# Taps to 128 partitions, a band in 128x32 tiles, first weights as fp32: the start of a convolution and gated feed-forward kernel

## The chip, the cores and the metric

The kernel runs on one core of a Trainium2 chip. The metric is the device time of one execution in microseconds. Before the change it is 761.82 us, the median of three runs (761.52 to 762.06). Beside the times there is a profile of one execution, taken by the hardware profiler.

## The reference

Two stages follow each other. The first is a causal convolution of seven taps over time, with one set of taps for each of 8 heads of 24 channels, the taps made to sum to one by a softmax. The second is a feed-forward block with a ReLU gate:

```python
w = weight - np.max(weight, axis=-1, keepdims=True)      # weight: 8 x 7
w = np.exp(w)
w = w / (np.sum(w, axis=-1, keepdims=True) + 1e-09)
x_pad = zeros of 6 steps ahead of x                       # x: 8 x 4096 x 192, fp32
out = np.einsum('hk,bskhg->bshg', w, x_unf)               # x_unf: 7 shifted views of x_pad
x = out.reshape(32768, 192)
gate = np.maximum(x @ w_gate, 0.0)                        # w_gate, w_val: 192 x 1536
val = x @ w_val
result = (gate * val @ w_out)                             # w_out: 1536 x 192
```

All inputs and the result are fp32.

## The kernel before, in words

**Tiling.** The batch is cut into two streams of four sequences, which lie in partitions 0 to 63 and 64 to 127; the 192 channels are three chunks of 64. A unit `u` is 1024 steps of both streams, two windows of 512 (`WIN`). There are 16 units. For each, `gate_val` (L601) runs over 12 blocks `f` of 128 columns of the gate and value weights: TensorE multiplies (L621), ScalarE takes the ReLU of the gate from PSUM (L632), VectorE multiplies by the value product (L633). Then `project_turn` (L636) multiplies by `w_out`, VectorE transposes out of PSUM (L661), and SyncE stores. The convolution of later units is done beside it by ScalarE, VectorE and GpSimd as seven scaled additions (`lane_first`, `lane_rest`, `product`, `add`).

**The first unit.** Its convolution can't wait for that lane, so TensorE does it, as a product of x with a band matrix: `band(h)` is 118 rows by 112 columns and holds the taps of head `h` along its diagonals. Window 0 is cut into five steps of 106 columns (`STEP`; the last has 88), each read from its own rows of x. `load_raw` (L106) requests the five loads of x for both streams as fp32, four by SyncE in the order 1, 0, 3, 4 and number 2 by ScalarE; `cast` (L118) turns them to fp16 on ScalarE in the order `STEPS0 = [1, 0, 2, 3, 4]`. `conv_steps` (L377) multiplies one step for one chunk of channels: eight small products in 128x32 tiles of the TensorE array. Chunk `c` needs heads up to 2, 5 and 7. The results are evicted from PSUM by `evict` (L401) into `dense[0]`, which the gate products of `f = 0` then read, chunk by chunk.

**The band.** The 8x7 taps are loaded into `w8` (L129). A product with `rows8` (L203), a 0/1 matrix made by GpSimd's `affine_select`, spreads each head's taps over 16 partitions into the PSUM tile `spread`. VectorE takes the maximum `mx` (L275), ScalarE the exponential `e` (L278) and the sum (L281), VectorE forms `prod`, `blk`, the reciprocal `sm` and three groups of `blocks` (L287 to L299), one group for heads 0 to 2, 3 to 5, and 6 to 7. TensorE raises each group to a band in PSUM, eight products of 128x128 a group (L335), each placed 16 steps further; zero products (L209) have cleared the banks. VectorE casts each band to fp16 (L343). GpSimd makes `wn`, the normalised taps (L308), for the lane's tap table, which SyncE then copies by small DMAs (L354).

**Idle products.** `hold` (L191) has TensorE multiply ones ahead of the first real work, in groups given by `WARM`: 13 times 128 columns before L203 and 9 times 128 after it.

**Weights.** Gate and value weights are cast to fp16 by GpSimd's DMAs (`load_w`, L221) in four groups of columns: 0 to 128, to 384, to 768, to 1536 (`CUTS`), gate and value alternating. They land in partitions 0 to 63; a copy to partitions 64 to 127 (`both_halves`, L229) is made by VectorE for the first two 128 columns, by GpSimd (`pool_halves`) for those to 1280, by SyncE's DMA for the rest. A one-element memset of `Wg` by VectorE (L178) stands ahead of GpSimd's first weight load, which writes over the same element and so waits for it.

**What sets the order.** Each engine runs its instructions in program order; the framework adds the semaphores. GpSimd's order is: small setup, weight groups 0 and 1, `wn`, weight groups 2 and 3, copies, the first stream of x for window 1 (`load_x(1, ...)`, L97), copies, the second stream, copies, and the loads of the lane. Window 1's convolution by TensorE comes after block `f = 9` of window 0 (`CONV1`). PSUM tiles named `ps` rotate through four buffers of two banks.

## Time and profile before

| | |
|---|---|
| median of 3 runs | 761.82 us |
| span of the profiled execution, first to last instruction | 760.2 us |
| granted TensorE clock, mean | 1.000 |
| TensorE busy | 756.0 us, 99% |
| VectorE, ScalarE, GpSimd busy | 675.8, 610.1, 461.3 us |
| first gate product (L621) starts | 7.81 us |
| convolution of window 1 (L391) starts | 20.96 us |
| HBM read and written | 28.98 and 25.17 MB |

The profiled execution has no other time of its own than its span, which is 1.6 us less than the median; what lies ahead of the first instruction and behind the last is not in it. In the views, PE is TensorE, PEld its weight load, DVE is VectorE, ACT ScalarE, POOL GpSimd and SP SyncE; a `q` behind the name marks the issue of a DMA. L12 is line 12 of the kernel before. A row of the timeline has start, duration, engine, line, operation, output and input, and in brackets how long the engine was idle and what it waited for. The chain of waits is followed back from the last instruction, at each step to what let it start. Busy shares are averages; where nearly all of the span is one engine's work, what is left to look at are the microseconds in which that engine does something else.

### The profile page before, as it was taken

How to read it: one execution, taken by the hardware profiler on the slowest of the kernel's cores; microseconds unless marked ns; L12 is line 12 of the kernel's file. 1: busy time of each engine (PE TensorE's matmuls, PEld its weight loads, DVE VectorE, ACT ScalarE, POOL GpSimd, SP SyncE). 2: the span in 40 equal slices, each digit the busy share in tenths (PEclk: the TensorE clock that was granted, in tenths of full speed). 3: DMA queues.
4: the chain of work that ended last, by engine and by line, in shares of the span. 5: the costliest groups of instructions: out<-in, count | busy, mean ns of one | idle time of the engine just before them, and what ended most of it. 6: DMA issues, size and time to landing. Idle time of an engine off the chain costs nothing.

```text
span 760.2 us, 30531 instructions
## 1 busy us (share of the span) xinstructions
PE 756.0 (99%) x13724; PEld 454.8 (60%) x13724; DVE 675.8 (89%) x647; ACT 610.1 (80%) x680; POOL 461.3 (61%) x311
## 2 busy tenths in 40 slices
PE   9999999999999999999999999999999999999998
PEld 5555555565565666656666565666656556566658
DVE  7889989998998989989999899998999989897891
ACT  7897887878878788887877878788797887877671
POOL 8729649195591946829377392874919659193600
PEclk9999999999999999999999999999999999999999
DMA  8953532345324443333434324352243531240302
GB/s 142 137 69 92 79 85 46 43 96 75 85 44 52 97 66 85 55 61 83 60 85 71 66 67 55 85 85 69 56 49 93 77 86 44 23 100 9 85 2 85
DMA packets 153714, 54.07 MB, mean 71 GB/s; under 512 B 148912, under 2 KB 153584, under 8 KB 153584
## 3 DMA queue, kind: packets, MB, share of 16 engines
q1 hardware_dynamic: 117376, 37.78, 21.6%
q0 software_dynamic: 35808, 14.07, 16.4%
q8 instruction: 107, 1.75, 1.0%
q10 hardware_dynamic: 400, 0.27, 0.1%
q14 instruction: 23, 0.19, 0.1%
HBM read 28.98 MB, written 25.17 MB: 71 GB/s over the span
## 4 chain that ended last, share of the span: by engine, by line
PE 99%; DMA 0%; ACT 0%; issue 0%
PE ps L621 65%; PE ps L643 31%; PE ps L686 2%; PE ps L391 0%; DMA w<-in_weight_dram 0%; PE ps L193 0%; PE ps L335 0%; PE ps L414 0%; PE ps L209 0%; PE ps L203 0%; ACT out_s L697 0%; ACT L127 0%
## 5 line engine op out<-in xcount | busy, mean ns | idle before, releaser
L633 DVE TENSOR_TENSOR hT<-gr,ps 128x1024 f16<-128x1024 f16 (+1 forms) x385 | 469.1, 1219 | 35.5 <-ACT gr L632 8.7
L632 ACT ACTIVATE gr<-ps 128x1024 f16<-128x1024 f32 (+1 forms) x385 | 392.8, 1021 | 114.4 <-PE ps L621 114.4
L550 POOL TENSOR_TENSOR prod<-prod,prod 128x896 f32<-128x896 f32 x145 | 302.6, 2087 | 251.8 <-DVE prod L584 242.7
L621 PE MATMUL ps<-xc,Wg 64*64 64x512 f16 (+1 forms) x4464 | 318.4, 376 | 0.0
L621 PE MATMUL ps<-xc,Wv 64*64 64x512 f16 (+1 forms) x4464 | 318.3, 376 | 0.0
L643 PE MATMUL ps<-hT,Wo 64*64 64x512 f16 x4320 | 235.8, 376 | 0.0
L621 PEld LDWEIGHTS <-Wv 64*64 64x64 f16 (+1 forms) x4464 | 149.9, 106 | 98.5 <-DVE hT L633 0.3
L621 PEld LDWEIGHTS <-Wg 64*64 64x64 f16 (+1 forms) x4464 | 145.4, 107 | 103.4 <-issue 0.2
L643 PEld LDWEIGHTS <-Wo 64*64 64x64 f16 x4320 | 137.3, 107 | 95.7
L538 ACT ACTIVATE prod<-x_r,tap 128x1024 f32<-128x1024 f16 (+2 forms) x195 | 182.7, 1017 | 0.0
L574 DVE SCALAR_TENSOR_TENSOR acc<-x_r,tap,acc 128x1024 f32<-128x1024 f16 (+3 forms) x150 | 118.0, 854 | 0.0
L661 DVE STREAM_TRANSPOSE out_s<-ps 128x1024 f32<-128x1024 f32 x45 | 56.2, 1248 | 28.4 <-PE ps L643 24.4
L550 POOL TENSOR_TENSOR xc<-prod,prod 128x896 f16<-128x896 f32 x29 | 60.6, 2089 | 2.3
L479 POOL COPY x_p<-x_e 128x1536 f16<-128x1536 f16 (+1 forms) x32 | 42.2, 1351 | 0.0
L251 POOL DMA_DIRECT2D x_e<-in_x_dram x30 | 26.6, 890 | 0.0
L574 DVE SCALAR_TENSOR_TENSOR xc<-x_r,tap,acc 128x1024 f16<-128x1024 f16 (+3 forms) x30 | 25.2, 840 | 0.0
L563 ACT ACTIVATE acc<-x_r,tap 128x1024 f32<-128x1024 f16 (+3 forms) x30 | 22.5, 800 | 0.0
L656 ACT COPY turned_by<-ps 128x2 f32<-128x2 f32 x45 | 7.0, 155 | 16.8 <-PE ps L643 14.8
L686 PEld LDWEIGHTS <-hT 128*128 128x128 f16 x192 | 15.8, 98 | 0.4 <-issue 0.4
L686 PE MATMUL ps<-Wo,hT 128*128 128x192 f16 x192 | 16.0, 246 | 0.0
L697 ACT COPY out_s<-ps 128x768 f32<-128x768 f32 (+2 forms) x5 | 3.2, 638 | 12.7 <-PE ps L686 12.7
L697 DVE COPY out_s<-ps 128x192 f32<-128x192 f32 x1 | 0.4, 359 | 13.3 <-PE ps L686 13.3
(61 smaller groups left out, 74.4 us busy)
## 6 DMA issues: line engine op xcount, KB each, us to landing
out_dram<-out_s SPq DMA_DIRECT2D x125, 192.0 KB
x_e<-in_x_dram POOLq DMA_DIRECT2D x28, 384.0 KB, 6.3
x_r<-x_p SPq DMA_TRANSPOSE x116
prod<-in_moe_w_out_dram POOLq DMA_DIRECT2D x1, 576.0 KB, 8.7
prod<-in_x_dram SPq DMA_DIRECT2D x3, 168.0 KB
out_dram<-out_s SPq DMA_DIRECT2D x5, 96.0 KB
out_s<-in_x_dram POOLq DMA_DIRECT2D x2, 210.0 KB, 6.2
out_s<-in_x_dram POOLq DMA_DIRECT2D x2, 192.0 KB, 6.1
```

Source lines behind the costliest of these rows:

```text
L251: nc.gpsimd.dma_start(out=xe[:, 0:n, st, :, :].rearrange("p j c r -> p j (c r)"), in_=bass.AP(tensor=x.tensor, offset=x.offset + row * D, ...
L479: nc.gpsimd.tensor_copy(out=xp[:, js, :, st, :], in_=xe[:, js, st, :, :])
L538: nc.scalar.activation(out=both(prods[b, k], b, at, n), in_=shifted(b, c, k, t, n), func=ACTF.Copy, scale=tap[:, c, k : k + 1],)
L550: nc.gpsimd.tensor_tensor(out=acc if k < KW - 1 else xcs[b][:, w, :, :].rearrange("p c t -> p (c t)")[:, LDVE : NCH * WIN], in0=acc, in1=p ...
L563: nc.scalar.activation(out=both(accs[b], b, at, n), in_=shifted(b, c, 0, t, n), func=ACTF.Copy, scale=tap[:, c, 0:1],)
L574: nc.vector.scalar_tensor_tensor(out=result(b, at, n) if k == KW - 1 else both(acc, b, at, n), in0=shifted(b, c, k, t, n), scalar=tap[:, c ...
L621: nc.tensor.matmul(out=pss[i][q : q + M, st, :], lhsT=W[64 * st : 64 * st + 64, c, 128 * f + q : 128 * f + q + M], rhs=xcb[64 * st : 64 * ...
L632: nc.scalar.activation(out=gr[:, sts], in_=pss[0][:, sts], func=ACTF.Relu)
L633: nc.vector.tensor_tensor(out=h[:, f, sts], in0=gr[:, sts], in1=pss[1][:, sts], op=ALU.mult)
L643: nc.tensor.matmul(out=ps[64 * st : 64 * st + 64, b, :], lhsT=Wo[64 * r : 64 * r + 64, f, p, :], rhs=hs[b][64 * r : 64 * r + 64, f, st, :] ...
L661: nc.vector.transpose(out=o[:].rearrange("p t (b d) -> p b t d", b=2)[:, :, :, 32 * p : 32 * p + 32], in_=ps[:].rearrange("p b (t c) -> p ...
L686: nc.tensor.matmul(out=ps[:, i // 2, D * (i % 2) : D * (i % 2) + D], lhsT=h[:, f, st, 128 * q : 128 * (q + 1)], rhs=Wo[:, f, :, :].rearran ...
```

## The change: what it does

- The taps are requested by one DMA straight into 128 partitions, each head's row repeated 16 times. `rows8`, its select and the product into `spread` go; `mx` and `e` read the loaded tile. The two groups of idle products become one of 22 times 128 columns.
- The band products write 32 partitions each, in 128x32 tiles, in the order `PLACED`, two for each group of 32 partitions.
- In the convolution of window 0, step 4 of chunks 0 and 1 comes after the four other steps of both. The evictions of chunks 0 and 1 are split at column 318 (`early_cols`, `late_cols`) between VectorE and ScalarE.
- The first 128 columns of both weights come as fp32 by four DMAs into `sent`, all 128 partitions, the gate's by SyncE and the value's by ScalarE, behind the loads of x. VectorE casts them into `Wg` and `Wv`. GpSimd no longer loads group 0; the memset's element moves to column 128, the first of group 1.
- The first stream of x for window 1 is requested after GpSimd's copies up to column 768 instead of after those up to 384.

```diff
-    WARM = [(4, 4, 4, 1), (4, 4, 1)]
+    WARM = (4, 4, 4, 4, 4, 2)
     STEPS0 = [1, 0, 2, 3, 4]
+    PLACED = [0, 2, 4, 6, 1, 3, 5, 7]
...
-    w8 = const.tile([H, KW], FP)
-    nc.scalar.dma_start(out=w8[:], in_=weight)
+    w = const.tile([128, KW], FP)
+    nc.scalar.dma_start(
+        out=w[:],
+        in_=bass.AP(
+            tensor=weight.tensor, offset=weight.offset, ap=[[KW, H], [0, 128 // H], [1, KW]]
+        ),
+    )
     for jj in (1, 0, 3, 4):
         load_raw(nc.sync, jj)
     load_raw(nc.scalar, 2)
+    sent = apool.tile([128, 2 * LPOOL], FP, name="prod6")[:, 0 : 2 * NCH * 128].rearrange(
+        "p (i c f) -> p i c f", i=2, c=NCH
+    )
+    for i, (queue, src) in enumerate(((nc.sync, moe_w_gate), (nc.scalar, moe_w_val))):
+        for half in (slice(0, 64), slice(64, 128)):
+            queue.dma_start(
+                out=sent[half, i],
+                in_=src.rearrange("(c p) f -> p c f", p=64)[:, :, 0:128],
+            )
...
-    rows8 = const.tile([H, 128], FP)
-    select(rows8[:], H, [[-1, H], [0, HR]])
...
-    nc.vector.memset(Wg[0:1, 0, 0:1], 0.0)
+    nc.vector.memset(Wg[0:1, 0, 128:129], 0.0)
...
-    spread = psum.tile([128, 2, 512], FP, name="ps")
-    hold(*WARM[0])
-    nc.tensor.matmul(out=spread[:, 0, 0:KW], lhsT=rows8[:], rhs=w8[:], start=True, stop=True)
-    hold(*WARM[1])
+    hold(*WARM)
...
-    for s in range(2):
-        load_w(s)
+    load_w(1)
...
-        out=mx[:], in_=spread[:, 0, 0:KW], axis=mybir.AxisListType.X, op=ALU.max, negate=True
+        out=mx[:], in_=w[:], axis=mybir.AxisListType.X, op=ALU.max, negate=True
     )
-    nc.scalar.activation(out=e[:, 0:KW], in_=spread[:, 0, 0:KW], func=ACTF.Exp, bias=mx[:])
+    nc.scalar.activation(out=e[:, 0:KW], in_=w[:], func=ACTF.Exp, bias=mx[:])
...
     pool_halves(2)
-    xts[1] = load_x(1, range(1))
     for s in (3, 4, 5):
         pool_halves(s)
+    xts[1] = load_x(1, range(1))
     load_x(1, range(1, 2))
...
-        for j in range(128 // HR):
+        for j in PLACED:
+            q = HR * j // 32 * 32
...
-                lhsT=Z[:, 112 - HR * j : 240 - HR * j],
+                lhsT=Z[:, 112 - HR * j + q : 144 - HR * j + q],
...
-                stop=(j == 128 // HR - 1),
+                stop=(j % 2 == 1),
+                tile_position=(0, q),
...
-    def evict(copy, g, ps, c):
-        copy(out=dense[0][:, g, c, :], in_=ps[:, 0, :])
+    def evict(copy, g, ps, c, cols=slice(0, WIN)):
+        copy(out=dense[0][:, g, c, cols], in_=ps[:, 0, cols])
...
-    for c, steps in ((0, STEPS0[:3]), (1, STEPS0[:2]), (0, STEPS0[3:]), (1, STEPS0[2:]), (2, STEPS0)):
+    for c, steps in ((0, STEPS0[:4]), (1, STEPS0[:4]), (0, STEPS0[4:]), (1, STEPS0[4:]), (2, STEPS0)):
         conv_steps(0, first[c], c, steps)
-    both_halves(nc.vector.tensor_copy, 0, Wg)
-    both_halves(nc.vector.tensor_copy, 0, Wv)
-    for c, copy in enumerate((nc.scalar.copy, nc.vector.tensor_copy, nc.scalar.copy)):
-        evict(copy, 0, first[c], c)
+    early_cols, late_cols = slice(0, 3 * STEP), slice(3 * STEP, WIN)
+    evict(nc.vector.tensor_copy, 0, first[0], 0, early_cols)
+    for i, dst in enumerate((Wg, Wv)):
+        nc.vector.tensor_copy(out=dst[:, :, 0:128], in_=sent[:, i])
+    evict(nc.scalar.copy, 0, first[0], 0, late_cols)
+    evict(nc.scalar.copy, 0, first[1], 1, early_cols)
+    evict(nc.vector.tensor_copy, 0, first[1], 1, late_cols)
+    evict(nc.scalar.copy, 0, first[2], 2)
```

More of the change, by code (lines that the diff above doesn't have):

```diff
@@ L335 @@
             nc.tensor.matmul(
-                out=part[:, 0 : SUB * n].rearrange("p (h t) -> p h t", t=SUB)[:, :, s0 + lo : s0 + hi],
-                lhsT=Z[:, 112 - HR * j : 240 - HR * j],
+                out=part[q : q + 32, 0 : SUB * n].rearrange("p (h t) -> p h t", t=SUB)[
+                    :, :, s0 + lo : s0 + hi
+                ],
+                lhsT=Z[:, 112 - HR * j + q : 144 - HR * j + q],
                 rhs=blocks[:, heads[0] : heads[0] + n, lo:hi],
                 start=False,
-                stop=(j == 128 // HR - 1),
+                stop=(j % 2 == 1),
+                tile_position=(0, q),
                 skip_group_check=True,
```

## The prediction

> **What bounds the kernel now.** I read the shares of the chain first, then the chain in order of time, then the timeline of the first 10 us.

> ```profile
> PE 99%; DMA 0%; ACT 0%; issue 0%
> ...
> 0.87 1.75 DMA w<-in_weight_dram
> 2.62 0.14 issue
> 2.76 0.56 PE ps L203 x2
> 3.32 1.07 PE ps L193 x3
> 4.39 0.75 PE ps L209 x3
> 5.14 1.05 PE ps L335 x24
> 6.19 1.61 PE ps L391 x120
> 7.80 0.00 issue
> 7.81 13.22 PE ps L621 x120
> 21.03 1.64 PE ps L391 x120
> ```

> The last chain is TensorE almost throughout, and from the first gate product (L621) at 7.81 us on there is nothing but products. So the end of the kernel moves with the moment at which the gate products can run. The whole change lies in the start before 7.81, plus one transfer that feeds 21.03. In the start, the taps `w` pass through a product (L203), six small VectorE and ScalarE steps, the band products (L335) and the convolution (L391). Their rows:

> ```profile
> 0.81 1.91 SPq L109 DMA_DIRECT2D prod<-in_x_dram  x4
> 0.87 0.59 ACTq L129 DMA_DIRECT2D w<-in_weight_dram  x1
> 1.50 0.34 ACTq L109 DMA_DIRECT2D prod<-in_x_dram  x1
> 2.47 0.06 DVE L178 MEMSET Wg<- 1x1 f16 x1
> 2.84 0.80 POOL L224 DMA_DIRECT2D Wg<-in_moe_w_gate_dram  x1 [0.55 <-DVE Wg L178]
> 3.35 0.17 DVE L275 TENSOR_REDUCE mx<-ps 128x1 f32<-128x7 f32 x1 [0.83 <-PE ps L203]
> 4.44 0.15 DVE L295 RECIPROCAL sm<-sm 128x1 f32<-128x1 f32 x1
> 4.63 0.67 DVE L299 SCALAR_TENSOR_TENSOR blocks<-blk,sm,mask 128x66 f16<-128x66 f32 x3
> 5.55 0.35 POOL L308 TENSOR_SCALAR wn<-e,sm 128x7 f32<-128x7 f32 x1
> 5.56 1.22 DVE L343 CAST band<-ps 128x336 f16<-128x336 f32 x3 [0.26 <-PE ps L335]
> 5.84 0.69 POOL L224 DMA_DIRECT2D Wg<-in_moe_w_gate_dram  x1
> 6.18 0.51 ACT L119 CAST out_s<-prod 96x384 f16<-96x384 f32 x1 [0.34 <-DMA prod<-in_x_dram]
> 6.81 0.39 DVE L231 COPY Wg<-Wg 64x384 f16<-64x384 f16 x1
> 7.17 0.58 ACT L402 CAST xc<-ps 128x512 f16<-128x512 f32 x1 [0.48 <-PE ps L391]
> 8.02 0.39 PE L621 MATMUL ps<-xc,Wv 64*128 64x512 f16 x2
> ```

> Three things meet before 7.81: the band (cast from 5.56), the fifth load of x (its cast waited for a DMA until 6.18) and the first 128 weight columns (copied from 6.81). The third view is that of the DMA queues, in stretches: from 0.8 to 4.4 us, 4.5 to 4.75, 4.75 to 5.75, 6.0 to 7.5, 7.4 to 9.3 and 9.3 to 12 us. q1 and q10 carry what SyncE and ScalarE request, q0 what GpSimd requests. Below them is the row of 4.0 to 4.5 us by engine, whose last numbers are granted clock, DMA share and GB/s.

> ```profile
> DMA packets 971, 0.69 MB, mean 192 GB/s; under 512 B 73, under 2 KB 971, under 8 KB 971
> ...
> q1 hardware_dynamic: 105, 0.08, 94.7%
> q0 software_dynamic: 3, 0.00, 3.0%
> ...
> q0 software_dynamic: 302, 0.07, 85.0%
> q1 hardware_dynamic: 63, 0.04, 14.9%
> ...
> q0 software_dynamic: 408, 0.19, 103.0%
> ...
> q0 software_dynamic: 385, 0.27, 103.8%
> ...
> q0 software_dynamic: 311, 0.39, 103.0%
> ...
> 4.00:4.50 0.50, 0.50 (x4) 0.29 (x3) 0.47 (x3) 0.50 (x4) 0.50 (x2) 1.00 1.04 347
> ```

> The reader is to see that the 16 DMA engines are full from about 2.5 us on, and that q1's flow breaks off when q0's packets come: 105 packets in a quarter of a microsecond, then 63 in the whole next one, which were the tail of the fifth x load.

> **The change part by part.**

> *Taps straight to 128 partitions.* Removed: one GpSimd select, the product pair L203 (0.56 plus 0.14 issue). Added: 128 small packets instead of 8 on ScalarE's queue. The landing was 2.62; it is not earlier, and 3.2 at the latest, if each of 16 packets an engine takes turns with one x packet (33 ns, below). I take 2.9, so `mx` starts at 2.95 instead of 3.35, the reciprocal ends at 4.2 instead of 4.59, and the third block ends near 4.9 instead of 5.30: 0.4 us.

> *Band in 128x32 tiles.* The same 24 products. The nearest row in that form is L391: 120 in 1.61 us, 13 ns each, against 44 ns for L335. At 13 to 44 ns they cost 0.3 to 1.05 us; I take 0.35, because the form is that of L391. They then end with the blocks, and VectorE casts the first band at 4.9 instead of 5.56, the last one by 6.1 instead of 6.78. Convolution could start at 5.4. Merging the two groups of idle products keeps their number (22 times 128 columns), and they end ahead of the blocks: nothing, unless the slow clock below. One buffer fewer in the PSUM rotation puts the convolution into buffers whose readers are done: nothing.

> *Late step of x last, with split evictions.* The copies move between ScalarE and VectorE in pieces of one 0.58 us eviction; they hide beside the wait for the fifth x load. Alone it is worth up to what that load delayed.

> *First weights as fp32.* This is the term that decides. GpSimd's two first loads (98 kB read each, fp32) go; four loads of 98 kB come on q1 and q10, and GpSimd's next two (columns 128 to 383, 196 kB of fp16) start first. Their issue costs SyncE and ScalarE two slots each of about 0.45 (1.91/4): SyncE's end at 3.6, before its tap requests need `wn`; ScalarE's end at about 2.7, before it needs `mx`. Both hide. VectorE's two copies become two casts of 128x384 from fp32, 0.4 each by L231 and L343: 0.1 us more. What doesn't hide is the transfer. By 4.4 us 0.69 MB had moved, which is the first four x loads (172 kB each), and nothing of the change makes them faster. After them stand the fifth x load, 147 kB or 12 packets an engine, and 393 kB of weights, 768 packets of 512 bytes or 48 an engine. At 347 GB/s these 541 kB take 1.56 us: the last lands at 5.97 if no other queue takes a turn.

> But q0 takes turns. GpSimd's first load is let go by the memset L178; with one select (0.3) fewer ahead of it it issues at 2.54 instead of 2.84. Before, q0's first three packets fall in 4.5 to 4.75, 1.8 after the issue; so now from 4.35 on, exactly when the weights are to flow. And `wn`, which held back GpSimd's third load until 5.84, is ready at about 4.3 to 4.65, so that load issues at 4.65 and its packets follow from 6.2 to 6.4. An x packet takes an engine 33 ns (242 packets in 0.5 us on 16 engines), a 512-byte one by bytes 22; I use 27 for the mix. A q0 packet takes 59 ns (408 in 1.5 us) for the second weight group, 79 (385 in 1.9) for the third, 139 (311 in 2.7) for the fourth. Strict turns, one for one: 24 turns with the second group, 24 x 86 = 2.1, to 6.5; 24 with the third, 24 x 106 = 2.5, to 9.0; the last 12 with the fourth, 2.0, to 11.0. If SyncE's and ScalarE's queues each have a turn: 24 x (54 + 59) = 2.7, to 7.1, and 12 x 106 = 1.3, to 8.4. If only the second group competes: 5.97 + 24 x 0.059 = 7.4. I take 8.6, near the middle of these, since the 63 packets of the tail show q1 slowed but not which of q1 and q10 would share. From the tail (q1's packets ended by 5.75) to the cast (6.18) was 0.4, so the gate weights are seen at 9.0, cast by 9.4, the value weights by 9.8, and the first value product starts at 9.85 instead of 8.02.

> [...]

> *Second block's x later.*

> ```profile
> 9.34 0.86 POOL L97 DMA_DIRECT2D out_s<-in_x_dram  x1
> 13.74 0.79 POOL L97 DMA_DIRECT2D out_s<-in_x_dram  x1
> ...
> DMA to landing us min/median/max: 5.3/6.1/7.2
> ```

> The first request moves from 9.34 behind six more copies, to about 13; the second stays near 13.8. Landing by 19.1 to 21.0, against the convolution at 21.03, which itself moves with the start. Nothing if the start is later; up to 0.7 us if it is earlier.

> *Sum.* Weights decide: +1.8 us (9.85 against 8.02). The gains of 0.4 and 0.65 in the band are earlier than that and vanish in it; the fifth x load, behind 12 weight packets an engine and under turns done at 6.5 (24 x 86 ns after 4.4), seen by 6.9, cast by 7.4, its 56 products of 13 ns done by 8.2, too. The profiled execution spans 760.2, 1.6 below the median of 761.82; I put the difference on the median: 763.6.

> **The rivals.**

> *The transfers are hidden* (not slower). If q1 and q10 have the engines to themselves until they are empty, the weights land at 5.97 and are seen by 6.4; VectorE is free of bands at 6.1 and of the early eviction at 6.65, casts until 7.05 and 7.45, and the first value product starts at 7.5 instead of 8.02. With 0.1 to 0.3 more from the shorter chain: -0.7, 761.1. For it: before, the fifth x load had nearly ended when q0 came. Against it: those 63 packets. It decides if the gate weights are seen before 7.2.

> *Only the second weight group competes.* Seen at 7.8, cast 8.2 and 8.6: +0.6, 762.4. For it: `wn` could come later than 4.65 if the taps land at 3.2.

> *Every turn is shared to the end.* 11.0 in the sum above: first value product at 12.25, +4.2, 766.0.

> *The clock falls back.* The row L193 shows 9 times 128 columns in 1.07 us, 1.1 columns a ns, while L621 has 512 columns, two at a time, 120 in 13.22 us: 2.3 columns a ns. The clock column reads 1.00 in both stretches, so it doesn't show this slow start. With products missing for 2 us ahead of the gates, the slow rate could return; one or two blocks of 12 products (1.32 us each) at half rate cost 1.3 to 2.6 more: about 765. [...] The trace of before has no such gap, so it can't show it.

> **How the numbers follow.** Weights late by turns (763.0 to 764.6): 0.40. Hidden: 0.24. Only the second group: 0.18. Shared to the end or the clock: 0.15. Anything else: 0.03. 0.2% is 1.5 us, about what a measurement of this kernel can tell from no change. Slower: 0.36 of the 0.40 and the 0.15, 0.51. Same: the rest of these, the 0.18 and most of the hidden case, 0.45. Faster by 1.5 us would need the first gate product at 6.3, ahead of the band's own chain: 0.04. The range from 760.9 to 765.8 leaves out part of the worst case and little below.

> **What would show it.** Right: the first gate product waits for VectorE's cast of `sent`, which waits for a DMA until 8.5 to 9.5; `mx` starts near 2.95; the band products take 0.3 to 0.4; q1 and q0 both busy from 4.4 to 8.5. Wrong: casts of `sent` that start as soon as VectorE is free, before 7; a first gate product ahead of 7.8; or the fifth x load as the last wait. A gap before 21 would be the second block's x.

## The result and the profile after

The kernel with the change takes 766.75 us (median of 5 runs, 765.86 to 767.37) against 761.82 us before: a ratio of 1.0053, with a 95% interval from 1.0041 to 1.0064. That is 4.9 us slower, and nearly all of it arises in the first 15 us. The profiled execution spans 765.7 us against 760.2 before, 5.5 more; it is the slowest of the five, 0.6 above their median.

The chain of waits of the kernel after, in order of time (start, length, engine, what):

```profile
1.27 4.70 DMA prod<-in_x_dram
...
5.99 0.61 ACTq L144
...
6.71 0.31 ACT e L287
...
9.06 1.77 PE ps L404 x69
...
11.87 14.53 PE ps L634 x120
26.40 1.52 PE ps L404 x119
```

The chain no longer passes through the taps. It passes through a load of x, then through a DMA request that ScalarE issues only at 5.99 (L144, the second of its two for the value weights), and then through the exponential `e`. The gate products, now L634, start at 11.87 instead of 7.81, 4.06 us later, and their first ten blocks take 14.53 instead of 13.22, 1.31 more. Window 1's convolution takes 1.52 instead of 1.64. The sum, 5.3, is the difference of the spans but for 0.2.

The rows of the timeline after, in order (start, duration; in brackets the idle time ahead of it and what ended it):

```profile
0.88 1.24 ACTq L130 DMA_DIRECT2D w<-in_weight_dram  x1
2.55 4.05 ACTq L144 DMA_DIRECT2D prod<-in_moe_w_val_dram  x2
5.27 0.16 DVE L284 TENSOR_REDUCE mx<-w 128x1 f32<-128x7 f32 x1 [3.04 <-DMA w<-in_weight_dram]
6.71 0.30 ACT L287 ACTIVATE e<-w,mx 128x7 f32<-128x7 f32 x1 [4.40 <-DMA prod<-in_x_dram]
8.15 0.65 PE L345 MATMUL ps<-blocks,Z 128*32 128x48 f16 x24 [4.06 <-DVE blocks L308]
8.50 1.22 DVE L356 CAST band<-ps 128x336 f16<-128x336 f32 x3
9.06 2.75 PE L404 MATMUL ps<-band,out_s 112*32 112x106 f16 x120 [0.26 <-DVE band L356]
10.86 0.49 DVE L415 CAST xc<-ps 128x318 f16<-128x318 f32 x1 [1.14 <-PE ps L404]
11.27 0.54 DVE L728 CAST Wg<-prod 128x384 f16<-128x384 f32 x1
11.39 1.14 ACT L415 CAST xc<-ps 128x194 f16<-128x194 f32 x3 [1.99 <-DVE xc L415]
11.87 0.61 PE L634 MATMUL ps<-xc,Wg 64*128 64x512 f16 x2
12.33 0.61 PE L634 MATMUL ps<-xc,Wv 64*128 64x512 f16 x2
12.73 0.63 PE L634 MATMUL ps<-xc,Wg 64*128 64x512 f16 x2
...
14.44 0.96 PE L634 MATMUL ps<-xc,Wg 64*128 64x512 f16 x6
14.55 1.64 POOL L98 DMA_DIRECT2D out_s<-in_x_dram  x2
```

Three rows of before, not shown yet, are needed beside them:

```profile
3.55 0.27 ACT L278 ACTIVATE e<-ps,mx 128x7 f32<-128x7 f32 x1 [1.25 <-DVE mx L275]
4.06 1.78 ACT L119 CAST out_s<-prod 112x384 f16<-112x384 f32 x4
6.12 1.68 PE L391 MATMUL ps<-band,out_s 112*32 112x106 f16 x120
```

From all these rows the delay of the first gate product can be split step by step:

| step | before | after | difference |
|---|---|---|---|
| taps landed, `mx` starts | 3.35 | 5.27 | +1.92 |
| from `mx` to `e` | 0.20 | 1.44 | +1.24 |
| from `e` to the first cast of a band | 2.01 | 1.79 | -0.22 |
| from that cast to the convolution | 0.56 | 0.56 | 0 |
| from the convolution to the first gate product | 1.69 | 2.81 | +1.12 |

Three things stand out. The taps land just before 5.27 instead of at 2.62. ScalarE has nothing to do and still runs `e` 1.44 us after `mx`: its idle time ended with a load of x, because the two requests L144 are spread over 4.05 us. In the trace the second of them waits for semaphore 104, which the load of x's step 0 and this request both signal: the last signal of that load comes at 5.97, and the request goes out at 5.99. And TensorE, which found nothing to do for 4.06 us, then runs the convolution in 2.75 instead of 1.68 us and starts its pairs of gate products 0.40 to 0.46 us apart, until 14.44; before, they came 0.21 to 0.25 apart from the first on. The view by stretches of time shows the granted TensorE clock beside this (the third number from the end of a row):

```profile
8.00:14.50 6.50, 6.03 (x158) 3.94 (x159) 4.20 (x12) 2.77 (x8) 6.41 (x13) 0.50 0.94 143
15.00:20.00 5.00, 5.00 (x50) 2.33 (x48) 4.54 (x5) 4.09 (x5) 4.50 (x9) 1.00 1.01 141
```

The DMA view shows where the taps' delay has its counterpart. It gives the GB/s that the 16 DMA engines moved, in 40 slices of 0.4 us over the first 16 us. Before:

```profile
GB/s 0 0 0 0 14 139 311 221 319 365 357 286 118 107 100 124 136 129 108 83 168 141 218 151 104 117 156 165 173 154 170 191 189 185 172 129 113 28 51 97
```

After:

```profile
GB/s 0 0 0 0 29 200 214 97 115 97 219 116 163 282 309 295 224 235 227 210 263 186 68 26 40 61 198 195 191 105 61 115 215 169 177 200 189 178 94 50
```

In the seven slices from 2.0 to 4.8 us, before sums to 1998 and after to 1058, which by 0.4 us is 0.80 against 0.42 MB. So the 16 DMA engines, which have the loads of x to move in both kernels, move about half as much while the 128 small packets of the taps are on their way. Four of the five loads of x are requested at about the same times as before; the fifth, ScalarE's, goes out at 2.15 instead of 1.50, because the taps' request ahead of it takes ScalarE 1.24 us instead of 0.59.

### The profile page after: what moved, and what is told of

It reads as the page before. It is cut to its first block, busy times and chain, and to the rows that moved or that the text cites. A ratio compares the mean times of both kernels' runs of the same rounds, so it can differ in the third digit from the quotient of the medians.

```text
span 765.7 us, 30530 instructions
## 1 busy us (share of the span) xinstructions
PE 757.2 (99%) x13721; PEld 426.1 (56%) x13721; DVE 676.6 (88%) x648; ACT 610.2 (80%) x681; POOL 459.5 (60%) x308
## 3 DMA queue, kind: packets, MB, share of 16 engines
q8 instruction: 107, 1.75, 0.9%
## 4 chain that ended last, share of the span: by engine, by line
PE 98%; DMA 1%; DVE 0%; issue 0%; ACTq 0%; ACT 0%; SPq 0%; DVEq 0%
PE ps L634 65%; PE ps L656 30%; PE ps L699 2%; DMA prod<-in_x_dram 1%; PE ps L404 0%; PE ps L427 0%; DVE blocks L308 0%; ACTq L144 0%; DVE Wg L728 0%; DVE band L356 0%; SPq L110 0%; DVE prod L296 0%; ACT out_s L710 0%; DVE blk L303 0%; ACT e L287 0%
## 5 line engine op out<-in xcount | busy, mean ns | idle before, releaser
L634 PE MATMUL ps<-xc,Wg 64*64 64x512 f16 (+1 forms) x4464 | 315.3, 377 | 0.1
L634 PE MATMUL ps<-xc,Wv 64*64 64x512 f16 (+1 forms) x4464 | 315.1, 377 | 0.0
L634 PEld LDWEIGHTS <-Wv 64*64 64x64 f16 (+1 forms) x4464 | 143.9, 106 | 105.1 <-DVE Wv L728 0.4
L634 PEld LDWEIGHTS <-Wg 64*64 64x64 f16 (+1 forms) x4464 | 133.7, 107 | 115.8 <-issue 1.0
L656 PEld LDWEIGHTS <-Wo 64*64 64x64 f16 x4320 | 126.4, 107 | 106.5
```

What stands on the lines that cost most here:

```text
L634: nc.tensor.matmul(out=pss[i][q : q + M, st, :], lhsT=W[64 * st : 64 * st + 64, c, 128 * f + q : 128 * f + q + M], rhs=xcb[64 * st : 64 * ...
L656: nc.tensor.matmul(out=ps[64 * st : 64 * st + 64, b, :], lhsT=Wo[64 * r : 64 * r + 64, f, p, :], rhs=hs[b][64 * r : 64 * r + 64, f, st, :] ...
```

## The experiments

All ratios are against the kernel before, run in the same session. The edit of each is shown against the kernel it starts from.

**The taps and ScalarE's queue: undo one, the other, both.** `old_taps` is the kernel after with the taps loaded and spread as before; `values_by_sync` is the kernel after with the value weights requested by SyncE, which leaves ScalarE free; `old_taps_values_by_sync` has both edits.

```diff
old_taps, against after:
-    WARM = (4, 4, 4, 4, 4, 2)
+    WARM = [(4, 4, 4, 1), (4, 4, 1)]
...
+    w8 = const.tile([H, KW], FP)
+    nc.scalar.dma_start(out=w8[:], in_=weight)
...
+    select(rows8[:], H, [[-1, H], [0, HR]])
...
+    nc.tensor.matmul(out=spread[:, 0, 0:KW], lhsT=rows8[:], rhs=w8[:], start=True, stop=True)
...
values_by_sync, against after:
-    for i, (queue, src) in enumerate(((nc.sync, moe_w_gate), (nc.scalar, moe_w_val))):
+    for i, (queue, src) in enumerate(((nc.sync, moe_w_gate), (nc.sync, moe_w_val))):
```

> The changed kernel with the taps loaded as 8 rows and spread by the product, as before; everything else of the change stays. Theory A (the request of 128 tiny packets is late, 5.24 instead of 2.62 us, and slows the x loads beside it): x loads come as before, mx starts near 3.35, the second value load on ScalarE's queue is let go when x step 0 has landed, near 4.1, so e starts near 4.8 instead of 6.71; first gate product near 8.3, 762 to 763. Theory B (the weight loads fill the queues, and the taps are only their victim): little changes, mx waits still, 765.5 or more.

> The changed kernel with the two value loads requested by SyncE behind the gate loads, so that ScalarE's queue has no request that waits. Theory A (with its second part: e was held from 5.43 to 6.71 by the request in front of it, which waited for x step 0): mx still near 5.3, e near 5.5, everything up to the first gate product 1.2 us earlier, at 10.7; 765.0 to 765.7. Rival (e would have waited anyway, for the band or the x casts behind it): no change, 766.7.

> Both of the two other runs together. Theory A: e at 3.55 as in the kernel before, the band faster by its tiles; first gate product between 7.0 and 8.0, 761.0 to 762.2. The prediction's own theory (the weights lose turns to GpSimd's queue): VectorE's casts of sent wait for a DMA until 8.5 to 9.5, 763 to 764.6.

Measured: `old_taps` 764.87 us, 1.0033 [1.0021, 1.0045]; `values_by_sync` 764.98, 1.0040 [1.0025, 1.0055]; `old_taps_values_by_sync` 763.95, 1.0027 [1.0015, 1.0040]. In the timeline of `old_taps`:

```profile
3.54 0.17 DVE L284 TENSOR_REDUCE mx<-ps 128x1 f32<-128x7 f32 x1 [1.01 <-PE ps L213]
4.16 0.60 ACTq L139 DMA_DIRECT2D prod<-in_moe_w_val_dram  x1
4.81 0.27 ACT L287 ACTIVATE e<-ps,mx 128x7 f32<-128x7 f32 x1 [2.50 <-DMA prod<-in_x_dram]
```

With the old taps `mx` is back at 3.54, but `e` still stands behind ScalarE's second request, which goes out at 4.16. In the timeline of `values_by_sync` it is the other way round:

```profile
4.73 0.16 DVE L284 TENSOR_REDUCE mx<-w 128x1 f32<-128x7 f32 x1 [2.49 <-DMA w<-in_weight_dram]
4.93 0.30 ACT L287 ACTIVATE e<-w,mx 128x7 f32<-128x7 f32 x1 [2.62 <-DVE mx L284]
```

`e` follows `mx` at once, and `mx` is late. Each of the two alone is enough to make the start late by about 2 us (first gate products at 9.94 and 10.09), so undoing one doesn't give back its own term in full. One reason is that TensorE runs at the low rate in these kernels too. In the timeline of `old_taps`:

```profile
7.13 2.75 PE L404 MATMUL ps<-band,out_s 112*32 112x106 f16 x120 [0.26 <-DVE band L356]
```

Its pairs of gate products are 0.40 to 0.46 us apart until 12.44, though TensorE never stood for more than 0.90 us after its first product, and the mean granted clock of this execution is 1.0. A granted clock of 1.00 therefore doesn't show the full rate in these traces: in the kernel before it reads 1.00 from 0.85 to 2.39 us as well, over idle products that run at 1.1 columns a ns. So the low rate stood in `old_taps` without a gap of 4 us, and part of several differences below is this rate and not the waits themselves. When the rate first rises differs between kernels with nearly the same start, and what sets that moment stays open. With its 764.87 us `old_taps` fits neither of the ranges expected of it. With both undone, in the timeline of `old_taps_values_by_sync`:

```profile
6.09 2.75 PE L404 MATMUL ps<-band,out_s 112*32 112x106 f16 x120 [0.36 <-DVE band L356]
...
9.00 0.55 DVE L728 CAST Wg<-prod 128x384 f16<-128x384 f32 x1 [0.62 <-DMA prod<-in_moe_w_gate_dram]
9.47 0.54 DVE L728 CAST Wv<-prod 128x384 f16<-128x384 f32 x1
9.61 0.39 PE L634 MATMUL ps<-xc,Wg 64*128 64x512 f16 x2 [0.77 <-DVE Wg L728]
10.07 0.39 PE L634 MATMUL ps<-xc,Wv 64*128 64x512 f16 x2
```

Here VectorE's cast of `sent` waits for the gate weights until 9.00, as the prediction had it for the change itself, and the first value product starts at 10.07. In the kernel after this cast waits for no DMA: it starts at 11.27, behind the early eviction on VectorE. The late weights are real, and the other delays hide them. The convolution ran at the low rate here as well and ended at 8.84, just ahead of the gate weights.

**Is it GpSimd's queue that makes the weights late?** `weights_gate_late` is `old_taps_values_by_sync` with the memset of `Wg` and `load_w(1)` put behind `mx`, so that GpSimd's first weight request goes out at 4.12 instead of 2.85.

```diff
-    nc.vector.memset(Wg[0:1, 0, 128:129], 0.0)
...
-    load_w(1)
...
+    nc.vector.memset(Wg[0:1, 0, 128:129], 0.0)
+    load_w(1)
     nc.scalar.activation(out=e[:, 0:KW], in_=spread[:, 0, 0:KW], func=ACTF.Exp, bias=mx[:])
```

> The run with old taps and all four fp32 weight loads by SyncE, with VectorE's memset and GpSimd's first load moved behind mx, so that this load issues near 3.9 instead of 2.85. Prediction's theory (the weights lose turns to GpSimd's packets): they are seen near 7.2 instead of 9.0, first gate product near 8.0 instead of 9.61, 762.0 to 763.0. Rival (the weights are late because their requests are issued late, the value loads at 4.2 and behind): still 8.5 or later, 763.5 to 764.2.

Measured: 764.04 us, 1.0024 [1.0014, 1.0034], the same as without the move. Its timeline:

```profile
8.41 0.54 DVE L727 CAST Wg<-prod 128x384 f16<-128x384 f32 x1
...
9.45 0.55 DVE L727 CAST Wv<-prod 128x384 f16<-128x384 f32 x1 [0.49 <-DMA prod<-in_moe_w_val_dram]
...
10.05 0.39 PE L633 MATMUL ps<-xc,Wv 64*128 64x512 f16 x2 [0.65 <-DVE Wv L727]
```

The gate weights are there before 8.41, about half a microsecond or more ahead of the 8.9 of the run without the move, so in these two traces GpSimd's packets had held them up. The value weights, which SyncE requests from 4.21 to 5.48, land only at 9.36 all the same, and the first value product comes at 10.05 instead of 10.07. So the later weights don't move with the start of GpSimd's second group; whether it is the order in SyncE's queue or the turns with GpSimd's later loads that sets them stays open.

**The taps alone, and what in them is slow.** `taps_alone` is the kernel before with nothing but the direct taps. `taps_sixteen` is the same with the order of the repeats turned round: 16 repeats of all 8 rows instead of 8 rows repeated 16 times each. Partition p then holds row p mod 8, so its convolution uses other heads' taps; the amount of work is the same. `taps_spare` is the kernel before, with the old taps in use, plus the direct request into a tile that nothing reads.

```diff
taps_alone, against before:
-    nc.scalar.dma_start(out=w8[:], in_=weight)
...
+            tensor=weight.tensor, offset=weight.offset, ap=[[KW, H], [0, 128 // H], [1, KW]]
...
taps_sixteen, against before:
+            tensor=weight.tensor, offset=weight.offset, ap=[[0, 128 // H], [KW, H], [1, KW]]
...
taps_spare, against before, behind the load of w8:
+    spare = const.tile([128, KW], FP)
...
+            tensor=weight.tensor, offset=weight.offset, ap=[[KW, H], [0, 128 // H], [1, KW]]
```

> The kernel before with only the taps requested straight to 128 partitions. Theory A: mx near 5.3 instead of 3.35, e at once behind it, everything behind 1.9 us later, and the first gate products at the slow rate if TensorE's gap is long enough, 1.3 more: 763.5 to 765.2. Theory B: within 0.4 us of before.

> The run with the taps alone, but the 128 packets are asked for in another order: 16 repeats outside, 8 rows inside, so that partition p gets row p mod 8 instead of p div 16; the convolution then uses other heads' taps, the work is the same. Theory A1 (the request is slow because its packets lie on only 8 of the 16 DMA engines, 16 each in turn with x packets): mx near 3.5 to 4.0 instead of 4.88, x loads less late, 763.5 to 764.8. Theory A2 (128 tiny packets are slow in whatever order): mx near 4.9, 765.5 to 766.3.

> The kernel before with one more request, behind that of the taps: the same 128 tiny packets into a tile that nobody reads. Theory A (these packets themselves slow the x loads beside them): the casts of x steps wait for DMAs, the fifth from 6.18 to near 7, 762.5 to 763.5 against 762.3. Rival (only waiting for them costs, the x loads in taps_alone were late for another reason): no change within 0.3.

Measured: `taps_alone` 765.95 us, 1.0047 [1.0030, 1.0064]; `taps_sixteen` 764.96, 1.0029 [1.0015, 1.0044]; `taps_spare` 766.23, 1.0052 [1.0038, 1.0065]. The first rows of the taps in `taps_alone` and then in `taps_sixteen`:

```profile
4.88 0.16 DVE L275 TENSOR_REDUCE mx<-w 128x1 f32<-128x7 f32 x1 [2.65 <-DMA w<-in_weight_dram]
```

```profile
4.79 0.16 DVE L275 TENSOR_REDUCE mx<-w 128x1 f32<-128x7 f32 x1 [2.56 <-DMA w<-in_weight_dram]
```

Nothing else of the change is needed for the taps to be late, and the two orders land within 0.1 us of each other. Their times, 3.6 and 2.3 us above before, have intervals that overlap. On how many of the 16 DMA engines the packets lie in the one order or the other no run shows; the 8 engines with 16 packets each, from which theory A1 expected `mx` at 3.5 to 4.0, were my assumption. Whatever the order changes there, it doesn't bring the taps back to where they were: `mx` starts at 4.88 and 4.79, in the kernel before at 3.35. Not all of the 3.6 us is the wait for the taps. In `taps_alone` the first pairs of gate products start 0.40 to 0.43 us apart, and later TensorE stands until 13.41 behind one of VectorE's copies of weights, which takes 3.01 us here and took 0.28 in the kernel before; why it is so long isn't shown:

```profile
10.34 3.01 DVE L231 COPY Wg<-Wg 64x384 f16<-64x384 f16 x1
```

In `taps_spare` the taps in use come 0.4 us later than in the kernel before (`mx` at 3.77), and the unread request still costs 3.5 us. Its timeline, and then its GB/s in slices of 0.4 us over the first 16 us:

```profile
8.03 1.34 ACT L119 CAST out_s<-prod 112x384 f16<-112x384 f32 x3 [2.64 <-DMA prod<-in_x_dram]
...
11.04 0.61 PE L628 MATMUL ps<-xc,Wg 64*128 64x512 f16 x2
```

```profile
GB/s 0 0 0 0 31 175 308 313 103 165 101 198 284 311 181 129 133 135 152 124 148 185 149 133 138 161 182 159 131 143 173 167 174 190 223 150 97 44 60 136
```

The third step of x, which ScalarE requests behind the unread packets, is cast at 8.03, where before all four first casts ran from 4.06 on without a gap, the third from 4.88. From 2.0 to 4.8 us the DMA engines move 0.55 MB instead of 0.80. So the small request doesn't only arrive late: it holds back the x loads around it. The 3.5 us are not that alone, since TensorE is at the low rate here too: its first pairs of gate products start 0.40 to 0.43 us apart.

**Repeated bytes, near bytes, or small packets?** Three more unread requests, all of the kernel before, all into 128 partitions: `spare_rows` reads 28 bytes each from 128 different rows of x, `spare_packed` 128 times 28 bytes that lie one behind the other in x, `spare_long` the same 768-byte row of x 128 times.

```diff
spare_rows:
+        in_=bass.AP(tensor=x.tensor, offset=x.offset, ap=[[D, 128], [1, KW]]),
...
spare_packed:
+        in_=bass.AP(tensor=x.tensor, offset=x.offset, ap=[[KW, 128], [1, KW]]),
...
spare_long:
+        in_=bass.AP(tensor=x.tensor, offset=x.offset, ap=[[0, 128], [1, D]]),
```

> The kernel before with an unread request of 128 packets of 28 bytes behind that of the taps, as in taps_spare, but from the first 28 bytes of 128 different rows of x, so that no byte is read twice. Theory S (small packets are slow whatever they read): the x loads fall behind as in taps_spare, step 2 cast near 8, 765.5 to 766.5. Theory R (the taps request is slow because 16 packets read the same few bytes): x casts as before, 762 to 763.

> The same with 128 pieces of 28 bytes that lie one behind the other in x (3.5 kB in all). Theory S: as taps_spare, 765.5 or more. Theory R: as before, 762 to 763. If the near neighbourhood of the bytes matters, and not the repetition: between, or as taps_spare while spare_rows is not.

> The same with 128 packets of 768 bytes that all read the first row of x. Theory R: slow, x step 2 cast at 7 or later, 764.5 or more. Theory S: it costs its 98 kB at the rate of the other loads, 0.3 us; 762.2 to 763.2.

Measured: `spare_rows` 763.30 us, 1.0014 [1.0003, 1.0026]; `spare_packed` 764.17, 1.0021 [1.0008, 1.0034], with runs from 762.64 to 765.56, which by time alone can't be told from `spare_rows`; `spare_long` 764.99, 1.0033 [1.0022, 1.0045]. The casts of the later steps of x, in the timelines of `spare_rows`, `spare_packed` and `spare_long` in this order:

```profile
6.27 1.34 ACT L119 CAST out_s<-prod 112x384 f16<-112x384 f32 x3 [1.54 <-DMA prod<-in_x_dram]
```

```profile
6.79 1.34 ACT L119 CAST out_s<-prod 112x384 f16<-112x384 f32 x3 [2.04 <-DMA prod<-in_x_dram]
```

```profile
6.93 1.34 ACT L119 CAST out_s<-prod 112x384 f16<-112x384 f32 x3 [1.78 <-DMA prod<-in_x_dram]
```

The first of these casts is the step that ScalarE requests behind the unread packets. The number and size of the packets are equal in `spare_rows`, `spare_packed` and `taps_spare`; what differs is where they read, how close together and, in `taps_spare`, from another tensor and in a pattern of 8 rows times 16. In these three traces, the further the addresses lie apart, the sooner the x that follows is there: 6.27 from distinct rows, 6.79 from neighbouring bytes, 8.03 from 8 rows of 28 bytes read 16 times each. Each of these times is from one trace, and the traces of `spare_rows` and `spare_long` are of the fastest of eight runs.

The medians, 0.8 against 3.5 us, can't be read as the price of the place alone, because behind that cast `taps_spare` runs at the low rate and the other three traces don't. The 104 products of convolution behind the late cast show it, in `spare_rows` and then in `taps_spare`:

```profile
6.83 1.81 PE L396 MATMUL ps<-band,out_s 112*32 112x106 f16 x104 [0.74 <-ACT out_s L119]
```

```profile
8.59 2.52 PE L398 MATMUL ps<-band,out_s 112*32 112x106 f16 x104 [1.51 <-ACT out_s L119]
```

With the first ten blocks of gate products, 13.83 us against 13.16 by the chain, that is 1.4 of the 3.1 us between the two profiled spans (764.4 and 761.3). The other 1.8 lie in the cast itself, 8.03 against 6.27. Against the 4.88 of the kernel before, 128 packets from distinct rows already make it 1.4 late, and the taps' packets 3.2. So some 1.4 us of the delay came with 128 small packets from distinct rows, and 1.8 more hang on what sets the taps' request apart. `spare_long` fits, with large packets and a single source: cast at 6.93, and 1.7 us above `spare_rows` by the medians, of which its 98 kB would explain 0.3 by the 347 GB/s that the kernel before moves from 4.0 to 4.5 us. These runs don't show by what mechanism the place matters, and none of them tells the two tensors `weight` and `x` apart.

**The clock.** `warm_long` is the kernel after with 80 idle products of 128 columns instead of 22, so that TensorE is busy to about 7 us.

```diff
-    WARM = (4, 4, 4, 4, 4, 2)
+    WARM = (4,) * 20
```

> The changed kernel with 80 instead of 22 times 128 columns of idle products, so that TensorE works through the wait for the taps (4.1 to 8.15 us). Theory C (after 4 us without products TensorE runs at half rate: convolution 2.75 instead of 1.68 us, first gate pairs 0.43 instead of 0.21 us apart): convolution near 1.7, gate pairs at 0.21 from the start, the 120 products of the first ten blocks in 13.2 instead of 14.5; 764.3 to 765.3. Rival (the slow products wait for evictions and casts, not for the clock): no change, 766 to 767.

Measured: 765.52 us, 1.0037 [1.0024, 1.0050]. Its timeline:

```profile
6.56 0.30 ACT L287 ACTIVATE e<-w,mx 128x7 f32<-128x7 f32 x1 [4.26 <-DMA prod<-in_x_dram]
...
8.86 1.60 PE L404 MATMUL ps<-band,out_s 112*32 112x106 f16 x120 [0.25 <-DVE band L356]
...
10.97 0.39 PE L634 MATMUL ps<-xc,Wg 64*128 64x512 f16 x2 [0.50 <-DVE Wg L728]
...
11.69 0.39 PE L634 MATMUL ps<-xc,Wg 64*128 64x512 f16 x2
11.90 0.39 PE L634 MATMUL ps<-xc,Wv 64*128 64x512 f16 x2
```

The convolution is back at 1.60 and the pairs are 0.21 apart as soon as their operands are there. From `e` to window 1's convolution it is 17.89 us (6.56 to 24.45) against 19.69 in the kernel after (6.71 to 26.40): the clock cost 1.80 us, and the time agrees, 3.2 us above before instead of 4.9. The mean granted clock of the execution is 1.0 here and 0.996 in the kernel after, where it reads 0.50 from 8 to 14.5 us. In the trace of the kernel after this comes with 4.06 us without a product: the clock is at 0.50 from just before 8 us on, the convolution takes 2.75 instead of 1.60, and the pairs come 0.43 apart instead of 0.21. How long a gap it takes for the clock to fall no run shows.

**The band, and what it is worth.** `band_alone` is the kernel before with the band in 128x32 tiles; `band_late` has the late step and the split evictions besides; `before_filled` and `band_filled` are the kernel before and `band_alone` with idle products of 16 and 12 times 128 columns instead of 13 and 9.

```diff
band_alone, against before:
-        for j in range(128 // HR):
+        for j in PLACED:
+            q = HR * j // 32 * 32
...
+                lhsT=Z[:, 112 - HR * j + q : 144 - HR * j + q],
...
+                tile_position=(0, q),
...
band_late, against before, besides:
+    evict(nc.vector.tensor_copy, 0, first[0], 0, early_cols)
...
+    evict(nc.scalar.copy, 0, first[0], 0, late_cols)
...
before_filled and band_filled:
-    WARM = [(4, 4, 4, 1), (4, 4, 1)]
+    WARM = [(4, 4, 4, 4), (4, 4, 4)]
```

> The kernel before with only the band products in 128x32 tiles. Prediction's step: band products in 0.35 instead of 1.05, first band cast 0.2 to 0.3 earlier; convolution then ends 0.2 earlier at most, 761.6 to 762.3 where the kernel before has 762.1. Rival (short products in a quarter of the array and the gap behind them leave TensorE at the slow rate): convolution near 2.7 instead of 1.68, 762.8 to 764.

> The kernel before with the band tiles, the late step of x last and the split evictions; taps and weights as before. If the clock holds: first gate product near 7.4 instead of 7.81, 761.3 to 762.0. If not: as the run with the band alone or 0.3 better.

> The kernel before with 16 and 12 instead of 13 and 9 times 128 columns of idle products, so that the gap before the taps' product closes. Theory C (the clock rises after some 3 us of unbroken products, at 3.9 in the run with long idle products): rises sometimes before 6.0, band and convolution faster, 761.6 to 762.2 against 762.3. Rival (the taps' product in the middle breaks it anyway, the longer idle products delay the zero products and the band): same or 0.3 slower.

> The kernel before with the band tiles and with 16 and 12 times 128 columns of idle products. Theory C: the band tiles gain what they did not show alone, because the convolution stays at full rate, 761.5 to 762.1. Rival: as the band tiles alone, 762.3.

Measured: `band_alone` 762.32 us, 0.9995 [0.9985, 1.0004]; `band_late` 763.02, 1.0005 [0.9995, 1.0014]; `before_filled` 762.49, 0.9998 [0.9989, 1.0007]; `band_filled` 762.23, 1.0002 [0.9993, 1.0010]. None can be told from no change. `before_filled` was to raise the rate sooner and didn't: its convolution takes 2.49 us. Two rows say more of the others. In `band_alone`'s profile the taps came 0.2 us later than in that of before and the convolution starts no earlier, at 6.19, and runs at the low rate; in `band_late`'s, ScalarE's piece of the split eviction waits for VectorE's:

```profile
6.19 2.75 PE L396 MATMUL ps<-band,out_s 112*32 112x106 f16 x120 [0.36 <-DVE band L348]
```

```profile
7.43 1.14 ACT L407 CAST xc<-ps 128x194 f16<-128x194 f32 x3 [0.89 <-DVE xc L407]
```

In `band_filled` the first gate product does come at 7.67, 0.14 before that of the kernel before; then, by the chain, TensorE stands at 12.80 behind GpSimd's copy of the second group of value weights, and window 1's convolution starts at 21.39 instead of 21.03. An earlier start runs into the next weights. So I found no version that beats the kernel before.

## Why the prediction was right or wrong

The direction held, and the kernel is slower by 4.9 where 1.8 us were forecast; the time lies 0.95 us above the top of the range. Step by step:

- **Taps straight to 128 partitions: wrong, and the step that failed first.** I put the landing at "3.2 at the latest, if each of 16 packets an engine takes turns with one x packet". It was about 5.25, and 4.7 to 4.95 in the other kernels that have it. That bound counted the packets that the request waits for, and no run shows how many of them lie on one engine: the 16 were my assumption. Nor did it count what the packets cost the others: with them on their way the DMA engines moved 0.42 instead of 0.80 MB, and `taps_spare` shows 3.5 us, low rate included, for a request that nobody reads. A bound on the price of an operation that the trace doesn't show was worked out from packets of another kind.
- **"Both hide", of the four weight requests: wrong for ScalarE.** I counted issue slots of 0.45 and not the wait ahead of one. The second request stood behind the load of x's step 0 and with it `e`: 1.24 us. `old_taps` has the same wait without the taps, `values_by_sync` hasn't got it.
- **Band products: right in size only without the low rate.** They took 0.65 instead of 0.35 in the kernel after and 0.35 in `band_filled`. The 0.22 gained from `e` to the cast vanishes, as said.
- **"They hide", of the split evictions: wrong, by a little.** From the first eviction to the gate product it is 1.01 us (10.86 to 11.87) against 0.64 before (7.17 to 7.81), since the cast of `Wg` waits its turn on VectorE and ScalarE's piece waits for VectorE's.
- **Weights by turns: right in itself, and not what decided.** With the two causes above taken out, the cast of `sent` waited until 9.00 (forecast: 9.0), the first value product came at 10.07 (9.85) and the time rose by 1.6 us (1.8), with the value weights requested by SyncE and not, as in the forecast, by ScalarE. In the change itself the weights were there before VectorE came to cast them at 11.27, so this term was hidden behind the ones I had at nothing. Its cause holds only for the gate half: `weights_gate_late` brings the gate weights earlier and not the value weights. And the 63 packets of q1, which I held against the case of hidden transfers, were the rest of one load and can't show how two full queues share. No run shows the strict turns that the sum was made of; what the runs show in their place is the 9.00 for the gate weights, and their being there before 8.41 once GpSimd's first request went out at 4.12 instead of 2.85.
- **Second block's x: right.** Its requests moved to 14.55, and no gap stands ahead of 26.40.
- **The rivals.** "The clock falls back" was the right mechanism and was put at 1.3 to 2.6 us; `warm_long` gives 1.8, and the granted clock, 1.00 in the kernel before, falls to 0.50 just before 8 us in the kernel after. It had a share of 0.15 with another case, because I let products be missing for 2 us, the weights' delay, where the taps and ScalarE's wait made it 4.06. "Every turn is shared to the end" named 766.0, near the result, but by a cause that the rows refute: the casts of `sent` waited for no DMA. "Hidden" and "only the second group" needed an early start and fell with it.

So the failed step is the price of the taps: the change's smallest item, 3.5 kB, was bounded so that it could not lose, and cost, with ScalarE's wait of 1.24 us and the 1.8 us of the low rate behind the gap, nearly all of the difference.

## What to carry to other kernels

Price a DMA that repeats a few source bytes over 128 partitions by its own trace and not by its size, and keep it away from the loads that a start hangs on; spreading a small load with one product on an idle TensorE was cheaper here by 3.6 us (`taps_alone`, with what the late start brought besides). Ahead of a request on an engine that computes, look for what the request itself has to wait for: in the kernel after, `e` behind it in program order waited with it, 1.24 us. When several small delays meet, ask how long TensorE is left with nothing, because in the kernel after the low rate behind a gap of 4.06 us cost 1.8 us more. Then look at how long the products themselves take: the low rate also stood in kernels whose breaks were under 1 us and whose mean granted clock was 1.0 (`old_taps`).

## What the runs showed that I had not expected

- One unread request of 128 times 28 bytes raises the time by 3.5 us when it repeats 8 rows, 1.7 when it reads bytes in a line and 0.8 when it reads 128 different rows; 128 times the same 768 bytes cost 2.5. The 3.5 holds some 1.4 us of the low rate of TensorE.
- With TensorE kept busy without a break from 0.85 us on (`warm_long`), its rate doubles at about 4 us: the idle products start 0.43 us apart until 3.79 and 0.22 apart from 4.13 on. In the kernel after, with the gap after 4.1, it is high again only from 14.4 on, 5.4 us after the convolution has begun.
- Requests on ScalarE's queue held the engine itself in the kernel after: 4.05 us for the two of the value weights (L144), while the same two took SyncE 1.95 in `values_by_sync`.
